# A planner's tables for a two-attention kernel: output products placed later, VectorE exps nearer to a phase's end, shared PSUM banks used sooner

## The chip, the cores and the metric

The kernel runs on one core of one Trainium2 chip. The metric is the device time of one execution in microseconds. Times are medians of several runs; a profile is of one execution, which has its own time.

## The reference

Two attention blocks read the same `x` (2048 rows, 512 columns) and are mixed by a gate that depends on the row. A has 32 query heads of width 16 on one shared key and value head; B has 32 full heads of width 16.

```python
g = sigmoid((x * gate_w).sum(-1, keepdims=True))
# A: q = x @ wq (32 heads of 16), k = x @ wk, v = x @ wv (one head of 16)
# B: q, k, v = split(x @ wqkv)     (32 heads of 16 each)
p = softmax(q @ k.T * 16 ** -0.5)  # for each head, 2048 x 2048
a, b = (p_A @ v_A) @ A_wo, (p_B @ v_B) @ B_wo
return g * a + (1 - g) * b
```

## The kernel before, in words

The exponentials of 2 x 32 x 2048 x 2048 scores are the bulk of the work. They are cut into **phases**: four groups of eight heads (`gi`), for each of them A and then B, two halves of the queries (`half`) and two pairs of head pairs (`q`): 32 phases, numbered from 0, of which 0 to 3 are A's, 4 to 7 B's, 8 to 11 A's, and so on. A phase has 32 **quads** of two **exps**, 64 exps in all, each of them 128 x 1024 elements.

One exp goes through these steps. TensorE makes its scores, 8 matmuls of 512 columns, into one of four PSUM tiles of two banks (`slots`). ScalarE reads it and writes exp into a tile in SBUF, `prob` or `vec` in the profile (L783, `exp`). When both exps of a quad are there, TensorE multiplies them with the values (L837, `values`) and adds up in the phase's own PSUM tile (`pair[0]`); a quad is multiplied whole (512 columns) or in two halves (256). The two tiles are then free again. When all 32 quads are in, VectorE copies the sum to SBUF (L905, in `emptied`), row sums go through DRAM to be inverted and spread (L648 to L673, `normalised`), and VectorE makes the normalised pair of 16-bit tiles `o16` (L681 to L687). `o16` has 8 buffers.

Part of the exps are made on VectorE instead (`vector_job`, `chain`): TensorE writes the scores into the shared PSUM tile (`pair[1]`), and VectorE works out a polynomial. For B that is a chain of three instructions (L1037, L1040, L1044) with two tiles, for A one of seven (L1004 to L1017) with three.

Other TensorE work shares `pair[1]`: projections of q, k and v for later phases (24 products each, with VectorE's evacuation at L487 and L490, and 16 DMAs on the SP and POOL queues at L422 that lay out q and k), and **output products** (`o_unit`): for each half and group, four units of 12 products of `o16` with the output weights, evacuated by VectorE (L599), and added to the output in DRAM by DMA. Those of the last group stay on the chip (L592).

The order of all this is fixed when the kernel is built. A planner inside the kernel (`_Plan`, `pe_step`) keeps a clock for each engine with costs from a table (`EXP`, `SCORES`, `HALF`, ...) and emits one instruction after another; on the chip each engine goes through its list in order and waits for semaphores. What the planner chooses hangs on these:

- `pick`: which exp VectorE gets next. While the exps left on ScalarE in this phase cost more than `CHAIN` and VectorE's own backlog, it is the last quad of this phase, otherwise the last one of the next phase.
- `vector_job`: the number of free tiles that it needs, `KEPT` of them a reserve; `spare_tiles` counts the free ones.
- `pe_step`: if more than `LEFT` tiles are free (`LEFT_END` near a phase's end), work in the shared tile goes first (`bursts`), otherwise products with the values.
- `due` times of projections and output products; a unit with the earliest goes first, and `hurry` holds back VectorE exps when `JOB` for each job leaves too little time.

After the last phase comes a **tail**: VectorE and ScalarE copy the last sum (L902, L903), ten DMAs move it about (L651), VectorE inverts and multiplies (L661, L679), and the last products and output DMAs follow.

Of the kernel before, what the change touches and what calls it, by code (L numbers as in the profile page):

```python
# [13 lines left out]
F16 = mybir.dt.float16  # L14
# [6 lines left out]
P = 128  # L21
# [26 lines left out]
SLACK, TIGHT, URGENT, SOON, AHEAD, LATER = 404, 404, 300, 500, 900, 3000  # L48
# [4 lines left out]
PROBS, VECS = 10, 6  # L53
LEFT, LEFT_END, KEPT, BEGIN = 3, 5, 3, 5
# [117 lines left out]
def _fast(ctx, tc, x, wq_a, wk_a, wv_a, wo_a, wqkv_b, wo_b, gate_w, out, flag):  # L172
# [397 lines left out]
    o16s = {}  # L570

    def o_unit(j, half, t, done, last):
# [16 lines left out]
        def finish(end):  # L589
            def take():  # L590
# [32 lines left out]
        due = 32 * (LASTS + half) if ends else 32 * (8 * j + 2 * half + 8)  # L623
        undone[j, half] = undone.get((j, half), 0) + 1
        return _Unit(jobs, finish, lambda now: all(made(("o16", n, half, q), math.inf) <= now and made(("wo", *groups[n]), math.inf) <= now for n, q in done)
# [4 lines left out]
    def normalised(n, half, q, raw, turned, now):  # L630
# [11 lines left out]
        if not ends:  # L642
# [4 lines left out]
            for which, count in heads:  # L647
                nc.sync.dma_start(held.rearrange("(e h) q -> h e q", e=2)[to : to + count], raw[which])  # L648
                to += count
        for m, (part, at, to, n_rows, e) in enumerate(moves):  # L650
            queues[m % len(queues)].dma_start(part[ROWS * e + to :][:n_rows], raw[at, e])  # L651
# [165 lines left out]
    def idle(now):  # L817
# [4 lines left out]
        return chained() > WORK + AHEAD + (EXTRA if half_vec else 0) or pick(now) is None or spare_tiles() < (0 if half_vec else KEPT) + 2  # L822
# [60 lines left out]
    def emptied(t):  # L883
# [16 lines left out]
        def take():  # L900
            if ph == LASTS:
                nc.vector.tensor_copy(state["raw"][:, 0], full[:, 0])  # L902
                nc.scalar.copy(state["raw"][:, 1], full[:, 1])  # L903
# [3 lines left out]
        def then(end):  # L907
# [4 lines left out]
            normalised(n, half, q, state["raw"], turned, end)  # L912
# [20 lines left out]
    def pick(now):  # L933
# [6 lines left out]
        need = CHAIN + plan.backlog(3)  # L940
# [11 lines left out]
    def pressing():  # L952
# [4 lines left out]
        return ph <= quads[min(at[0], len(quads) - 1)][0] and left_in(ph) * EXP < CHAIN  # L957
# [4 lines left out]
    def vector_job(now):  # L962
# [6 lines left out]
        if u is None or spare_tiles() < (3 if source(quads[u // 2][0]) == "a" else 2) + (0 if half_vec else 1 if source(quads[u // 2][0]) == "a" else KEPT):  # L969
            return None  # L970
# [735 lines left out]
```

## Time and profile before

| | |
|---|---|
| time, median of 3 runs (lowest, highest) | 1768.24 us (1766.13, 1768.64) |
| the profiled execution: its time, its span | 1765.05 us, 1763.3 us |
| TensorE matmul busy | 1712.2 us (97%) |
| ScalarE busy | 1703.4 us (97%); 1840 exps at L783 |
| VectorE busy | 1314.0 us (75%) |
| GpSimd busy | 190.8 us (11%) |
| mean granted TensorE clock | 0.995 |

The time stands 1.75 us above the span of the same execution, which is counted from the first to the last instruction. The profiled execution is 3.2 us faster than the median of the three runs. Busy time is a union: instructions of an engine that overlap are counted once. One L783 lasts 1117 ns in the mean, but the next begins before it ends. A row of the timeline gives the start, the duration to the end of the last of a group, the engine, the line, and in brackets how long the engine had been idle and what ended that.

### The profile page before, as it was taken

The page shows a single profiled execution, that of the slowest core. Times are in us where ns is not written, and L with a number is a line of the kernel's source. Part 1 is how long each engine was busy: PE and PEld are TensorE (multiplying, and loading weights), DVE is VectorE, ACT ScalarE, POOL GpSimd, SP SyncE. Part 2 cuts the span into 40 slices and gives each one's busy share as a digit, 9 for nine tenths or more (in the row PEclk, how much of TensorE's full clock was granted, in tenths as well). Part 3 has the DMA queues.
Part 4 walks back from the last instruction along what each step waited for, and adds up shares of the span by engine and source line. Part 5 has one row for each costly group of instructions (what it writes and reads, how often), then busy time and mean ns, then how long its engine had stood idle before and what let it go on. Part 6 is the DMA issues. An engine that isn't in the chain of part 4 may idle for free.

```text
span 1763.3 us, 108947 instructions
## 1 busy us (share of the span) xinstructions
PE 1712.2 (97%) x50939; PEld 983.3 (56%) x50939; DVE 1314.0 (75%) x1504; ACT 1703.4 (97%) x1855; POOL 190.8 (11%) x314
## 2 busy tenths in 40 slices
PE   8999999999999999999999999999999999999996
PEld 5556554565555565546565556555565555555553
DVE  5458699986748784997687785699587687498944
ACT  5999999999999999999999999999999999999994
POOL 1102000000000101001211211000211221100000
PEclk9999999999999999999999999999999999999998
DMA  5212110113111222112323222111322322111311
GB/s 151 62 41 65 52 38 19 41 35 76 45 50 48 54 67 62 28 31 53 52 53 65 52 60 58 47 28 41 71 35 52 59 59 71 39 35 28 109 62 64
DMA packets 71152, 95.10 MB, mean 54 GB/s; under 512 B 27581, under 2 KB 36061, under 8 KB 70693
## 3 DMA queue, kind: packets, MB, share of 16 engines
q1 hardware_dynamic: 53892, 58.61, 12.3%
q0 software_dynamic: 13568, 27.22, 7.6%
q8 instruction: 401, 6.57, 1.5%
q10 hardware_dynamic: 3232, 2.23, 0.4%
q14 instruction: 59, 0.48, 0.1%
HBM read 23.45 MB, written 17.81 MB: 23 GB/s over the span
## 4 chain that ended last, share of the span: by engine, by line
PE 67%; ACT 19%; DVE 7%; issue 3%; DMA 1%; SPq 1%; ACTq 0%; DVEq 0%
PE slot L837 34%; PE slot L752 20%; PE slot L215 12%; ACT prob L783 12%; ACT vec L783 7%; DVE prob L1037 1%; DVE prob L1040 1%; DVE prob L1017 1%; DVE prob L1044 1%; DVE vec L1044 0%; DVE vec L1037 0%; DVE prob L1004 0%; SPq L673 0%; PE slot L1395 0%; PE slot L309 0%
## 5 line engine op out<-in xcount | busy, mean ns | idle before, releaser
L783 ACT ACTIVATE prob<-slot 128x1024 f32<-128x1024 f32 x1118 | 1123.7, 1117 | 15.5 <-PE slot L752 14.4
L783 ACT ACTIVATE vec<-slot 128x1024 f32<-128x1024 f32 x712 | 749.9, 1119 | 5.3 <-PE slot L752 2.6
L837 PE MATMUL slot<-prob,vA 64*32 64x256 f32 (+1 forms) x7424 | 510.1, 451 | 0.1
L837 PE MATMUL slot<-prob,vB 64*32 64x256 f32 (+1 forms) x7480 | 499.8, 448 | 0.1
L752 PE MATMUL slot<-Qa,kA 64*32 64x512 f16 x8192 | 434.9, 379 | 6.6 <-DMA Qa<-loqa 2.2
L752 PE MATMUL slot<-Qb,K 64*32 64x512 f16 x8192 | 405.4, 379 | 25.0 <-ACT vec L783 9.7
L837 PE MATMUL slot<-vec,vB 64*32 64x256 f32 (+1 forms) x4840 | 373.9, 445 | 0.1
L837 PE MATMUL slot<-vec,vA 64*32 64x256 f32 (+1 forms) x4672 | 373.2, 445 | 0.2
L752 PEld LDWEIGHTS <-K 64*32 64x32 f16 x8192 | 187.2, 90 | 275.0 <-issue 212.4
L752 PEld LDWEIGHTS <-kA 64*32 64x32 f16 x8192 | 195.6, 90 | 247.7 <-issue 180.6
L837 PEld LDWEIGHTS slot<-prob,vA 64*32 64x32 f32 x7424 | 200.9, 106 | 42.3 <-issue 9.0
L837 PEld LDWEIGHTS slot<-prob,vB 64*32 64x32 f32 x7480 | 196.6, 106 | 48.4 <-issue 12.4
L837 PEld LDWEIGHTS slot<-vec,vB 64*32 64x32 f32 x4840 | 141.9, 106 | 27.5 <-issue 6.6
L837 PEld LDWEIGHTS slot<-vec,vA 64*32 64x32 f32 x4672 | 141.1, 106 | 26.6 <-issue 5.0
L1037 DVE TENSOR_SCALAR prob<-slot 128x1024 f32<-128x1024 f32 x92 | 112.7, 1225 | 19.8 <-PE slot L752 10.7
L1017 DVE SCALAR_TENSOR_TENSOR prob<-prob,prob 128x1024 f32<-128x1024 f32 x76 | 92.6, 1221 | 0.7
L1017 DVE SCALAR_TENSOR_TENSOR vec<-vec,prob 128x1024 f32<-128x1024 f32 x62 | 75.5, 1221 | 0.6
L215 PEld LDWEIGHTS <-o 64*32 64x32 f16 x3072 | 51.4, 93 | 36.2 <-ACT o L684 7.4
L1004 DVE TENSOR_SCALAR prob<-slot 128x1024 int32<-128x1024 f32 x42 | 51.3, 1222 | 26.7 <-PE slot L752 21.9
L215 PE MATMUL slot<-w16ob,o 64*32 64x512 f16 x1536 | 62.6, 387 | 7.9 <-ACT o L684 5.7
L905 DVE COPY prob<-slot 128x1024 f32<-128x1024 f32 x20 | 24.5, 1223 | 56.3 <-PE slot L215 35.4
L1044 DVE SCALAR_TENSOR_TENSOR prob<-prob,prob 128x1024 f32<-128x1024 f32 x54 | 66.1, 1226 | 0.3
(187 smaller groups left out, 1670.9 us busy)
## 6 DMA issues: line engine op xcount, KB each, us to landing
vB<-vB SPq DMA_DIRECT2D x32, 192.0 KB
prob<-back SPq DMA_DIRECT2D x160, 32.0 KB
out_dram<-prob POOLq DMA_DIRECT2D x40, 128.0 KB, 4.3
xT<-out_dram SPq DMA_DIRECT2D x16, 256.0 KB
out_dram<-vec POOLq DMA_DIRECT2D x24, 128.0 KB, 4.5
out_dram<-xT SPq DMA_DIRECT2D x12, 256.0 KB
vec<-back SPq DMA_DIRECT2D x88, 32.0 KB
vec<-in_A_x_dram SPq DMA_DIRECT2D x10, 256.0 KB
```

Of the source, the lines that this page charges most:

```text
L215: nc.tensor.matmul(outs[n : n + COLS, i], lhs[i][rows(i), n : n + COLS], rhs[i][rows(i)], start=start, stop=stop)
L752: nc.tensor.matmul(bank[a : a + COLS, hh], k[rows(hh), key : key + COLS], Q[src, gi, half, p][rows(hh), j * BLK : (j + 1) * BLK], start=Tr ...
L783: nc.scalar.activation(probs[u], sc, AF.Exp, scale=SCALE / (UP * UP))
L837: nc.tensor.matmul(pair[0][32 * k : 32 * k + 32, i, cols], v[rows(i)], probs[2 * m + k // 2][rows(i), hh, cols], start=first, stop=last)
L905: nc.vector.tensor_copy(state["raw"], full)
L1004: nc.vector.tensor_scalar(tile("p").bitcast(I32), pair[1], SCALE / (UP * UP) / math.log(2) * 2.0 ** 23, None, op0=ALU.mult)
L1017: nc.vector.scalar_tensor_tensor(p, m if i == 3 else p, VEC[i], m if i else w, op0=ALU.add, op1=ALU.mult)
L1037: nc.vector.tensor_scalar(tile("p"), pair[1], CUBE[0] * SCALE / (UP * UP), CUBE[1], op0=ALU.mult, op1=ALU.add)
L1040: nc.vector.scalar_tensor_tensor(tile("w"), tiles["p"], CUBE[2], tiles["p"], op0=ALU.add, op1=ALU.mult)
L1044: nc.vector.scalar_tensor_tensor(p, w, CUBE[3], p, op0=ALU.add, op1=ALU.mult)
```

## The change

It changes the planner's numbers and three of its rules:

- **Output products.** Their due time (all but the last group's) moves by three phases, from `8 * j + 2 * half + 8` to `+ 11`. Since `o16` tiles are then read later, `readers` counts the units that still have to read each, and VectorE's copy into a new `o16` (`high`) is not emitted before the tile's earlier content has been read.
- **VectorE exps.** `CHAIN` becomes 20000 for A and 7000 for B, from 24000 for both; `KEPT` becomes 1, from 3; for A the reserve of one tile is kept. `JOB` goes from 900 to 500.
- **Shared banks.** `LEFT` becomes 1, from 3: work in the shared tile goes first while two tiles or more are free. In the last phase it was 1 already.
- **Due times of projections**: q 8000 ahead of its phase instead of 14000, v 24000 instead of 18000; k and v may begin 12 quads later. `idle` loses `AHEAD`.
- **Tail.** The last sum is copied into two tiles, one for VectorE's half and one for ScalarE's.

```diff
-SLACK, TIGHT, URGENT, SOON, AHEAD, LATER = 404, 404, 300, 500, 900, 3000
+SLACK, TIGHT, URGENT, SOON, LATER = 404, 404, 300, 500, 3000
-PROBS, VECS = 10, 6
-LEFT, LEFT_END, KEPT, BEGIN = 3, 5, 3, 5
+PROBS, VECS, O16 = 10, 6, 8
+LEFT, LEFT_END, KEPT, BEGIN = 1, 5, 1, 5
...
+    def read16(k):
+        return k < 0 or readers.get(made16[k], 1) == 0
...
-        due = 32 * (LASTS + half) if ends else 32 * (8 * j + 2 * half + 8)
+        due = 32 * (LASTS + half) if ends else 32 * (8 * j + 2 * half + 11)
...
-                e = plan.vec(lambda c=c: high(c), 200, 3.3, 0.0, (b,), None, due)
+                e = plan.vec(lambda c=c: high(c), 200, 3.3, 0.0, (b,), None, due, room=lambda: read16(before))
...
-        return chained() > WORK + AHEAD + (EXTRA if half_vec else 0) or pick(now) is None or spare_tiles() < (0 if half_vec else KEPT) + 2
+        return chained() > WORK + (EXTRA if half_vec else 0) or pick(now) is None or spare_tiles() < (0 if half_vec else KEPT) + 2
...
             if ph == LASTS:
+                state["other"] = free_tiles.pop()
                 nc.vector.tensor_copy(state["raw"][:, 0], full[:, 0])
-                nc.scalar.copy(state["raw"][:, 1], full[:, 1])
+                nc.scalar.copy(state["other"][:, 1], full[:, 1])
...
-        need = CHAIN + plan.backlog(3)
+        need = CHAIN["ab".index(source(ph))] + plan.backlog(3)
...
-        if u is None or spare_tiles() < (3 if source(quads[u // 2][0]) == "a" else 2) + (0 if half_vec else 1 if source(quads[u // 2][0]) == "a" else KEPT):
+        if u is None or spare_tiles() < (3 if source(quads[u // 2][0]) == "a" else 2) + (0 if half_vec else KEPT):
...
-    CHAIN, EARLY = 24000, 12
-    JOB, AFTER, TURN, SPARE, WORK, EXTRA = 900, 3000, 3000, 5000, 1500, 7000
+    CHAIN, EARLY = (20000, 7000), 12
+    JOB, AFTER, TURN, SPARE, WORK, EXTRA = 500, 3000, 3000, 5000, 1500, 7000
...
-        bursts = begins and spare_tiles() > 1 or at[0] < len(quads) and spare_tiles() > (1 if at[0] >= 32 * LASTS else LEFT_END if ending else LEFT)
+        bursts = begins and spare_tiles() > 1 or at[0] < len(quads) and spare_tiles() > (LEFT_END if ending and at[0] < 32 * LASTS else LEFT)
...
-                                     lambda s=s: starts_in(64 * s) - 14000))
+                                     lambda s=s: starts_in(64 * s) - 8000))
...
-                        units.append(project(part, "b", gi, half, part + "_b", past(m - 22 + 10 * half),
-                                             lambda m=m, half=half, ns=14000 if part == "k" else 18000: starts_in(m + 128 + 16 * half) - ns))
+                        units.append(project(part, "b", gi, half, part + "_b", past(m - 10 + 10 * half),
+                                             lambda m=m, half=half, ns=14000 if part == "k" else 24000: starts_in(m + 128 + 16 * half) - ns))
```

What it does to the programs, counted in their instructions: ScalarE has 1820 exps instead of 1840. VectorE has 162 of B's chains instead of 142, and 66 of A's as before. TensorE does the same scores, products and projections; 42 more quads are multiplied in two halves instead of whole (336 more matmuls). GpSimd and SP have as many instructions as before. B's chains were 4 to 14 in a phase and are now 6 to 14. The table below is counted from the built orders: exps on VectorE in each phase of the four B blocks, and the number of ScalarE exps of the same phase that are still to come in the order when the scores of the phase's last VectorE exp are made.

| phases | VectorE exps before | after | still to come before | after |
|---|---|---|---|---|
| 4 to 7 | 8, 12, 12, 6 | 12, 12, 10, 10 | 29, 32, 33, 32 | 9, 7, 21, 15 |
| 12 to 15 | 4, 12, 12, 6 | 14, 6, 10, 12 | 30, 34, 34, 32 | 12, 14, 25, 3 |
| 20 to 23 | 4, 14, 12, 4 | 12, 6, 10, 12 | 32, 25, 25, 34 | 13, 11, 25, 3 |
| 28 to 31 | 4, 14, 10, 8 | 12, 6, 12, 6 | 32, 19, 33, 24 | 13, 13, 15, 23 |

VectorE's order where phase 15 ends (the last of a B block; `L905 COPY`, in the new numbering `L916 COPY`, is the copy of the phase's sum). L1004 to L1017 and, in the new numbering, L1015 to L1028 are A's chain; L599 is the evacuation of an output product. Before:

```order
L1017 SCALAR_TENSOR_TENSOR prob_101<-prob_101,vec_106 128x1024
L599 TENSOR_SCALAR prob_105<-slot_79 128x1024
L1004 TENSOR_SCALAR vec_108<-slot_79 128x1024
L1008 TENSOR_SCALAR prob_100<-vec_108 128x1024
L1012 TENSOR_SCALAR vec_111<-vec_108 128x1024
L1017 SCALAR_TENSOR_TENSOR vec_108<-prob_100 128x1024
L1017 SCALAR_TENSOR_TENSOR vec_108<-vec_108,prob_100 128x1024
L905 COPY prob_103<-slot_81 128x1024
```

After; L1048, L1051 and L1055 are B's chain:

```order
L1051 SCALAR_TENSOR_TENSOR prob_104<-vec_108 128x1024
L1055 SCALAR_TENSOR_TENSOR vec_108<-prob_104,vec_108 128x1024
L1048 TENSOR_SCALAR vec_110<-slot_79 128x1024
L1051 SCALAR_TENSOR_TENSOR prob_104<-vec_110 128x1024
L1015 TENSOR_SCALAR prob_101<-slot_79 128x1024
L1055 SCALAR_TENSOR_TENSOR vec_110<-prob_104,vec_110 128x1024
L1015 TENSOR_SCALAR prob_99<-slot_79 128x1024
L1019 TENSOR_SCALAR prob_96<-prob_101 128x1024
L1019 TENSOR_SCALAR vec_106<-prob_99 128x1024
L1023 TENSOR_SCALAR prob_104<-prob_101 128x1024
L916 COPY prob_97<-slot_81 128x1024
```

Before, the chains ahead of the copy belong to the next phase, A's; now the phase's own last chain ends five instructions ahead of the copy of its sum.

VectorE's order where phase 20 ends (the first of a B block). Before:

```order
L1037 TENSOR_SCALAR prob_98<-slot_80 128x1024
L1040 SCALAR_TENSOR_TENSOR prob_96<-prob_103 128x1024
L1040 SCALAR_TENSOR_TENSOR vec_106<-prob_98 128x1024
L905 COPY prob_99<-slot_81 128x1024
L1044 SCALAR_TENSOR_TENSOR prob_103<-prob_96,prob_103 128x1024
```

After; L605 is the evacuation of an output product, L691 to L697 make an `o16`:

```order
L691 TENSOR_TENSOR vec_107<-vec_107 128x256
L1048 TENSOR_SCALAR vec_111<-slot_81 128x1024
L1055 SCALAR_TENSOR_TENSOR prob_100<-vec_110,prob_100 128x1024
L1051 SCALAR_TENSOR_TENSOR prob_102<-vec_111 128x1024
L1055 SCALAR_TENSOR_TENSOR vec_111<-prob_102,vec_111 128x1024
L605 TENSOR_SCALAR vec_110<-slot_82 128x1024
L916 COPY prob_99<-slot_79 128x1024
L694 CAST o_26384<-prob_101 128x256 x2
```

The output products of a second half, which stood in the A phases ahead, now stand from the end of phase 19 to phase 21, and the `o16` copy (L694) comes after the product.

ScalarE's order at the end of the last phase. Before:

```order
L783 ACTIVATE vec_111<-slot_81 128x1024
L783 ACTIVATE prob_97<-slot_82 128x1024
L903 COPY prob_103<-slot_80 128x512
L651 DMA prob_100<-prob_103 32x512
L651 DMA prob_100<-prob_103 16x512 x2
```

After:

```order
L793 ACTIVATE vec_111<-slot_79 128x1024
L793 ACTIVATE prob_99<-slot_80 128x1024
L914 COPY prob_96<-slot_81 128x512
L659 DMA prob_103<-prob_101 32x512
L659 DMA prob_103<-prob_101 16x512
L659 DMA prob_103<-prob_96 16x512
```

VectorE's copy goes to `prob_103` before, as ScalarE's does, and to `prob_101` after, another tile than ScalarE's `prob_96`.

More of the change, by code (lines that the diff above doesn't have):

```diff
@@ L589, in finish @@
         def finish(end):
+            for n, q in done:
+                readers[n, half, q] -= 1
             def take():
@@ L622, in o_unit @@
         jobs = [(lambda k=k: job(k), PRODUCT) for k in range(len(steps))]
-        due = 32 * (LASTS + half) if ends else 32 * (8 * j + 2 * half + 8)
+        due = 32 * (LASTS + half) if ends else 32 * (8 * j + 2 * half + 11)
         undone[j, half] = undone.get((j, half), 0) + 1
+        for n, q in done:
+            readers[n, half, q] = readers.get((n, half, q), 0) + 1
         return _Unit(jobs, finish, lambda now: all(made(("o16", n, half, q), math.inf) <= now and made(("wo", *groups[n]), math.inf) <= now for n, q in done)
@@ L647, in normalised @@
             for which, count in heads:
-                nc.sync.dma_start(held.rearrange("(e h) q -> h e q", e=2)[to : to + count], raw[which])
+                nc.sync.dma_start(held.rearrange("(e h) q -> h e q", e=2)[to : to + count], raw[0][which])
                 to += count
         for m, (part, at, to, n_rows, e) in enumerate(moves):
-            queues[m % len(queues)].dma_start(part[ROWS * e + to :][:n_rows], raw[at, e])
+            queues[m % len(queues)].dma_start(part[ROWS * e + to :][:n_rows], raw[e][at, e])
         if not ends:
@@ L654, in normalised @@
         plan.sp = max(plan.sp, now) + (len(moves) + 3) * ISSUE_SP
-        returns.append((plan.sp + LANDS, raw))
-        o16 = ops.tile([P, 2, BLK], F16, tag="o16", name=f"o16{n}{half}{q}", bufs=8)
+        returns.append((plan.sp + LANDS, raw[0]))
+        o16 = ops.tile([P, 2, BLK], F16, tag="o16", name=f"o16{n}{half}{q}", bufs=O16)
         o16s[n, half, q] = o16
+        made16.append((n, half, q))
+        before = len(made16) - 1 - O16
         cut = P if ends else BLK // 2
@@ L911, in then @@
                 free["pv"] = end + FROM_VEC
-            normalised(n, half, q, state["raw"], turned, end)
+            normalised(n, half, q, [state["raw"], state.get("other", state["raw"])], turned, end)
             parts = [(m, r) for m, r in ((n - 1, 0), (n - 1, 2), (n, 0), (n, 2))]
@@ L956, in pressing @@
         ph = quads[half_vec[0] // 2][0]
-        return ph <= quads[min(at[0], len(quads) - 1)][0] and left_in(ph) * EXP < CHAIN
+        return ph <= quads[min(at[0], len(quads) - 1)][0] and left_in(ph) * EXP < CHAIN["ab".index(source(ph))]
     def chained():
```

2 lines of the change are left out of this document (1 added, 1 removed).

## The prediction

> **What bounds the kernel now.** I read the page's busy times first, then the busy time in windows of 100 us, then the groups and single stretches of the timeline. The page:
>
> ```profile
> span 1763.3 us, 108947 instructions
> PE 1712.2 (97%) x50939; PEld 983.3 (56%) x50939; DVE 1314.0 (75%) x1504; ACT 1703.4 (97%) x1855; POOL 190.8 (11%) x314
> ```
>
> TensorE and ScalarE are both at 97%, so the page alone doesn't say which one sets the pace. The windows do (columns: PE, PEld, DVE, ACT, POOL busy, then clock and DMA):
>
> ```profile
> 100.00:200.00 100.00, 99.37 (x3132) 59.08 (x3131) 76.59 (x91) 99.29 (x109) 10.40 (x18) 1.00 0.20 52
> 200.00:300.00 100.00, 97.99 (x2848) 54.17 (x2840) 87.34 (x93) 99.82 (x110) 8.53 (x16) 1.00 0.15 39
> 300.00:400.00 100.00, 95.93 (x2848) 55.29 (x2833) 90.04 (x94) 99.87 (x110) 4.69 (x9) 1.00 0.13 34
> ...
> 600.00:700.00 100.00, 98.81 (x3080) 60.55 (x3072) 61.95 (x75) 98.11 (x108) 14.18 (x26) 1.00 0.21 57
> ...
> 900.00:1000.00 100.00, 99.88 (x3064) 58.90 (x3056) 71.86 (x83) 99.94 (x110) 18.73 (x24) 1.00 0.28 55
> ...
> 1100.00:1200.00 100.00, 96.09 (x2749) 51.81 (x2733) 84.13 (x86) 99.93 (x110) 6.34 (x12) 1.00 0.13 35
> ```
>
> ScalarE does 108 to 110 exps in each 100 us and is idle for at most 2 us, also at 300 and at 1100 us, where TensorE has 300 matmuls fewer to do than at 900. An exp does not get shorter where TensorE has less work, so ScalarE is the bound. The same asked for phases 4 to 28 as one window, ScalarE's exps alone, then all engines in the last 61 us before the last values end:
>
> ```profile
> 256.00:1584.00 1328.00, 1322.25 (x1438) 1.00 0.21 50
> ...
> 1681.00:1742.00 61.00, 59.10 (x1760) 33.19 (x1759) 24.75 (x27) 53.54 (x58) 0.00 (x0) 1.00 0.13 39
> ```
>
> In the long window an exp costs 1328 / 1438 = 0.9235 us, waits included. In the last 61 us ScalarE is busy for 53.5 and TensorE for 59.1: there the bound is TensorE. How full TensorE really is, its jobs tell. From the timeline near the end:
>
> ```profile
> 1733.53 0.42 PE L752 MATMUL slot<-Qb,K 64*32 64x512 f16 x8
> 1733.75 0.85 PE L215 MATMUL slot<-w16oa,o 64*32 64x512 f16 x24
> 1734.40 0.41 PE L752 MATMUL slot<-Qb,K 64*32 64x512 f16 x8
> 1734.62 1.05 PE L837 MATMUL slot<-prob,vB 64*32 64x512 f32 x16
> 1735.48 0.41 PE L752 MATMUL slot<-Qb,K 64*32 64x512 f16 x8
> ```
>
> From start to start, the scores of an exp take 0.22 us, three products 0.65, a quad with the values 0.86: one job of 8 matmuls is 0.215 us, a quad is four of them. The built program has 2048 + 4 x 1024 + 1152 (projections and output products) = 7296 jobs, 1569 us, 89% of the span.
>
> **The change part by part.** *Twenty exps leave ScalarE.* 20 x 0.9235 = 18.5 us off the path; by the window at 900 us, where ScalarE never pauses, 20 x 100 / 110 = 18.2. I take 18.5.
>
> *They come to VectorE*, as twenty more of B's chains of three:
>
> ```profile
> 1657.96 1.22 DVE L1037 TENSOR_SCALAR prob<-slot 128x1024 f32<-128x1024 f32 x1
> 1659.09 1.22 DVE L1044 SCALAR_TENSOR_TENSOR vec<-vec,vec 128x1024 f32<-128x1024 f32 x1
> 1660.22 1.22 DVE L1040 SCALAR_TENSOR_TENSOR prob<-prob 128x1024 f32<-128x1024 f32 x1
> ```
>
> From start to start 1.13 us, so 20 x 3 x 1.13 = 68 us; VectorE goes from 1314 to 1382 us of about 1747 (79%). The window at 300 us ran at 90% without a loss on ScalarE. Cost 0, as long as the idle 21% lies where it is needed; the other case is the first rival.
>
> *TensorE's jobs* are the same ones. Forty-two quads are cut in two, which costs nothing: halves are two jobs each, as long as the whole. 0 us.
>
> *Where its jobs stand* changes. The windows with few matmuls (300 and 1100 us) lie in the first two phases of a B block, which had few projections and output products or none. In the last three blocks they get some, so TensorE is filled evenly. ScalarE's idle time in such windows is 0.07 to 0.18 us; in fuller ones it is 0.06 (at 900) to 1.89 (at 600). Six phases, some 300 us, become full: at least 0, at most 3 x 1.8 = 5.4 us. I take 1.1, nearer to the window at 900, since the fullest of these phases has 237 jobs to 58 exps, as phase 16 (884 to 937 us) had before.
>
> *Tiles.* With less reserve, an exp may need a tile whose last reader, a quad with the values, stands behind its own scores in TensorE's order. Fifteen exps did, 23 do. ScalarE's waits of before:
>
> ```profile
> ACT prob L783 <- PE slot L752: 14.4, 18, 5.9
> ...
> ACT vec L783 <- PE slot L837: 0.6, 3, 0.2
> ```
>
> Waits for values were 0.6 us in all, 0.2 the longest. Eight more cost 0.3 to 1.6 us by that row; two of the 23, in the last phase, have 5 and 8 jobs behind them, 1.1 and 1.7 us. I take 0.8, between 0 and 3.2.
>
> *The last phase.* Behind the 58th-last exp TensorE had 267 jobs left, now it has 271: 4 x 0.215 = 0.9 us in a stretch where it is the bound. Behind the 120th-last there are 13 more: at most 2.8. I take 0.9. [...]
>
> *The tail.* Two copies of the last sum follow each other:
>
> ```profile
> 1742.02 0.69 DVE L902 COPY prob<-slot 128x512 f32<-128x512 f32 x1 [9.90 <-PE slot L837]
> 1742.74 2.42 SPq L651 DMA_DIRECT2D prob<-prob  x4
> 1742.75 0.59 ACT L903 COPY prob<-slot 128x512 f32<-128x512 f32 x1 [5.64 <-DVE prob L902]
> ```
>
> ScalarE waits for VectorE only because both write one tile. With two, its copy starts some 0.7 us earlier, and the last of the DMAs with it, unless the issue of four DMAs on SP (2.42 us) holds them. Between 0 and -0.7; I take -0.4. The Trainium skill (PSUM — Partial Sum Buffer, "Specifications (TRN2)") gives both engines full bandwidth on PSUM at once when the banks differ, as these two do; no run here shows it.
>
> *Due times.* Q comes later, and nothing is added for it: see the second rival. The wait that the check of `o16` adds is one of the planner: VectorE's list holds the copy further back, and what stands behind it is in another order, not stopped.
>
> Sum: -18.5 + 1.1 + 0.8 + 0.9 - 0.4 = -16.1. The profiled execution of 1765.05 would come to 1749; its span to 1747.2. The median stands 3.2 us higher than that execution, so I predict 1768.24 - 16.1 = 1752 us.
>
> **The rivals.** *A phase's end waits for VectorE (slower).* The last VectorE exp of a B phase was scored 19 to 34 ScalarE exps before the phase's end, now it is 3 to 25 (the table of the change). In the orders, ten more of the B phases end on a quad that VectorE made. If VectorE is late there, the sum is closed late, and ScalarE, which is 2 to 9 exps into the next phase by then (14 after phase 30), runs out of tiles. VectorE is stopped by DMAs:
>
> ```profile
> DVE each L664 <- DMA each<-held: 13.9, 7, 4.3
> ...
> 1597.00 0.35 DVE L664 RECIPROCAL each<-each 128x32 f32<-128x32 f32 x1 [2.02 <-DMA each<-held]
> ...
> 1599.90 0.41 PE L752 MATMUL slot<-Qb,K 64*32 64x512 f16 x8 [1.77 <-DVE prob L1037]
> ...
> 1601.02 2.10 ACT L783 ACTIVATE prob<-slot 128x1024 f32<-128x1024 f32 x2 [1.52 <-PE slot L752]
> ```
>
> Seven waits, 2.0 us in the mean, and the one that ended at 1597 us did reach ScalarE, by way of a late chain and TensorE: 1.5 us. At 2.0 us for each of the ten ends it would cost 20, and 1772 comes out. It decides from 1.6 us an end on. Against it: seven in 32 phases is not ten in ten, an A phase's end is mostly of that kind already, and the window at 900 us, in A, is ScalarE's best. Chance 0.10.
>
> *Q lands late.* In the order, the last product of the queries for a B block's second half stood 73 or more exps ahead of their first score; in the blocks at phases 12, 20 and 28 it is 13, 23 and 22 now. The time they need, in the trace:
>
> ```profile
> L487 DVE TENSOR_SCALAR hiqb<-slot 128x1024 f16<-128x1024 f32 x8 | 9.8, 1222 | 19.1 <-ACT prob L783 12.7 <-PE slot L215 6.4
> ...
> 691.56 0.54 POOL L422 DMA_DIRECT2D Qb<-hiqb  x1 [12.38 <-DVE hiqb L487]
> ...
> 694.86 0.59 SPq L422 DMA_DIRECT2D Qb<-loqb  x1
> ...
> DMA to landing us min/median/max: 2.0/2.8/4.1
> ```
>
> VectorE's evacuation of 1.2 us ends as the first issue starts at 691.56, so the queries were through TensorE near 690; to 694.86 + 4.1 = 699 it is 9 us for the first two tiles, and 13 exps are 12 us. With 3 us of waiting on SP and POOL the first is late; all three, by 3 us each, give 1752 + 9 = 1761. Most of it speaks against: 22 exps are 20 us. Chance 0.14 for a gain of 3.5 to 10 us, by this or by full windows, tiles and the last phase at their upper ends (5.4, 3.2 and 2.8: also 1761).
>
> *TensorE takes over.* If 97% busy meant full, nothing would be gained: 1768. Against it are the 89% in jobs and the windows with fewer matmuls. Chance 0.08, with all else that ends within 0.2%.
>
> That the change does not do what it says is excluded: the 20 exps are counted.
>
> **How the numbers follow.** The forecast, a gain of 10 to 25 us, gets 0.68. With the second rival's 0.14 that is 0.82 for faster by more than 0.2% (3.5 us, about what a measurement of this kernel can tell from none); 0.08 within; 0.10 slower. The low end of the range: all 18.5, 0.7 of the tail and a third of the 14.4 us that ScalarE waited for scores, -24, so 1744. The high end: full windows at 5.4, tiles at 3.2, the last phase at 2.8 and one late Q at 3 give -18.5 + 14.4 = -4.1, so 1764; no change and slower lie beyond.
>
> **What the profile after would show.** The exp line with 1820 instructions and ScalarE's busy time down by about 18 us; 256 to 1584 us still at 0.92 us an exp; B's chains at 162 each; the windows in second phases of B with as many matmuls as the others. ScalarE's copy of the last sum would start with VectorE's. I am wrong if ScalarE's idle time grows by 10 us or more: behind scores with Qb (late Q), behind values or by VectorE's chains at the ends of B's phases.

## The result and the profile after

The changed kernel takes 1752.73 us (median of 4 runs, 1751.99 to 1753.65), the kernel before 1767.77 us (4 runs): 15.0 us less, ratio 0.9916, 95% interval [0.9899, 0.9933]. The forecast was 1752 us. The profiled execution of after has a span of 1750.1 us, 13.2 us less than the one of before; the rest of the difference is the spread of single executions. One execution in the whole study, of `short_both`, took 2120 us at a granted clock of 0.751, and the times and ratios below leave it out.

The page of after, busy times and the two groups of ScalarE's exps (count, busy and mean duration, then idle time ahead of them and what ended it):

```profile
span 1750.1 us, 110408 instructions
PE 1711.5 (98%) x51611; PEld 1006.9 (58%) x51611; DVE 1382.3 (79%) x1564; ACT 1685.4 (96%) x1835; POOL 192.4 (11%) x314
...
L793 ACT ACTIVATE prob<-slot 128x1024 f32<-128x1024 f32 x1100 | 1095.7, 1105 | 18.6 <-PE slot L762 14.5 <-PE slot L847 2.3 <-DVE vec L1051 0.3
L793 ACT ACTIVATE vec<-slot 128x1024 f32<-128x1024 f32 x710 | 736.0, 1105 | 6.8 <-PE slot L762 4.7 <-DVE xT L598 1.3 <-issue 0.3
```

ScalarE's busy time went from 1703.4 to 1685.4 us and VectorE's from 1314.0 to 1382.3. The 1810 exps here and ten whose tiles bear other names are the 1820. TensorE's busy time is as before, in a shorter span.

The windows that were shown of before, as far as they tell something, with the long one and the last 64 us before the last values end (columns as before: PE, PEld, DVE, ACT, POOL, clock, DMA):

```profile
300.00:400.00 100.00, 95.86 (x2658) 50.63 (x2648) 89.15 (x94) 99.34 (x110) 4.13 (x8) 1.00 0.14 34
...
700.00:800.00 100.00, 98.70 (x3036) 59.79 (x3027) 82.89 (x94) 98.79 (x108) 9.69 (x18) 1.00 0.25 64
...
900.00:1000.00 100.00, 99.65 (x3117) 57.85 (x3104) 79.87 (x93) 99.90 (x110) 13.39 (x18) 1.00 0.23 48
...
1100.00:1200.00 100.00, 98.87 (x3053) 60.22 (x3045) 79.07 (x90) 97.69 (x107) 17.53 (x26) 1.00 0.28 57
1500.00:1600.00 100.00, 98.96 (x3084) 60.65 (x3084) 77.12 (x89) 98.86 (x108) 19.99 (x28) 1.00 0.31 60
...
1665.00:1729.00 64.00, 62.30 (x1812) 36.43 (x1796) 32.17 (x34) 54.95 (x60) 0.00 (x0) 1.00 0.12 37
256.00:1584.00 1328.00, 1315.31 (x40120) 771.53 (x40119) 1098.70 (x1202) 1317.39 (x1433) 150.14 (x235) 1.00 0.22 49
```

In the long window an exp now costs 1328 / 1433 = 0.9267 us; it was 0.9235. That is 0.0032 x 1433 = 4.6 us of new waiting. The window at 1100 us shows where: the first two phases of a B block, which had 2749 matmuls in 100 us and 110 exps on ScalarE, have 3053 matmuls and 107 exps. The windows at 700 and 1500 us, in the other two late B blocks, look alike: ScalarE is idle for 1.2 and 1.1 us, at 1100 for 2.3. In the first B block (300 us), which got no output products, little changed: 2658 matmuls instead of 2848, and 0.66 us of idle time instead of 0.13.

Worked out from the starts of ScalarE's exps, phase by phase, these rows hold nearly all of the difference. The other phases are between 2.2 us shorter (phase 11) and 0.8 us longer at that price, and come to -0.4:

| stretch | before | after | at 0.9235 us an exp, after is |
|---|---|---|---|
| phases 12, 13, 20, 21, 28, 29 | 307.5 us for 332 exps | 308.8 us for 328 | 5.1 us too long |
| phases 30 and 31 | 104.6 us for 110 | 105.5 us for 110 | 1.0 us too long |
| phases 0 to 3 | 228.9 us for 244 | 227.6 us for 244 | 1.3 us shorter |
| first exp to last exp | 1708.3 us for 1840 | 1694.3 us for 1820 | 4.4 us too long |

So 20 x 0.9235 = 18.47 us less and 4.43 more, -14.0 between the first and the last exp; the first exp starts 0.7 us later, and from the last exp on there is 0.1 us more: -13.2.

Of the six phases of the first row, 12, 20 and 28 lost nothing against before (-0.2, +0.1 and -0.3 us), and 13, 21 and 29 lost 1.3, 3.2 and 0.9. Yet TensorE had no less to do in the first three: its matmuls in the trace, at the prediction's 0.215 us a job, fill 94 to 95% of phases 12, 20 and 28 and 89 to 92% of 13, 21 and 29.

### The profile page after: what moved, and what is told of

Read it like the earlier page. It is cut to its first block, busy times and chain, and to the rows that moved or that the text cites. A ratio compares the mean times of both kernels' runs of the same rounds, so it can differ in the third digit from the quotient of the medians.

```text
span 1750.1 us, 110408 instructions
## 1 busy us (share of the span) xinstructions
PE 1711.5 (98%) x51611; PEld 1006.9 (58%) x51611; DVE 1382.3 (79%) x1564; ACT 1685.4 (96%) x1835; POOL 192.4 (11%) x314
## 4 chain that ended last, share of the span: by engine, by line
PE 70%; ACT 19%; DVE 4%; issue 4%; DMA 1%; SPq 1%; ACTq 0%; DVEq 0%; POOL 0%
PE slot L847 36%; PE slot L762 21%; PE slot L215 12%; ACT prob L793 11%; ACT vec L793 8%; DVE prob L1048 1%; DVE vec L1028 0%; DVE prob L1028 0%; ACT early L793 0%; DMA each<-held 0%; PE slot L1406 0%; PE slot L309 0%; DVE vec L1048 0%; DMA Qa<-loqa 0%; DVE xT L1544 0%
## 5 line engine op out<-in xcount | busy, mean ns | idle before, releaser
L793 ACT ACTIVATE prob<-slot 128x1024 f32<-128x1024 f32 x1100 | 1095.7, 1105 | 18.6 <-PE slot L762 14.5
L793 ACT ACTIVATE vec<-slot 128x1024 f32<-128x1024 f32 x710 | 736.0, 1105 | 6.8 <-PE slot L762 4.7
L847 PE MATMUL slot<-prob,vB 64*32 64x256 f32 (+1 forms) x7824 | 523.3, 441 | 0.8 <-issue 0.7
L847 PE MATMUL slot<-prob,vA 64*32 64x256 f32 (+1 forms) x7544 | 483.3, 439 | 0.4 <-issue 0.4
L762 PE MATMUL slot<-Qb,K 64*32 64x512 f16 x8192 | 422.3, 379 | 13.1 <-ACT vec L793 3.1
L847 PEld LDWEIGHTS slot<-prob,vB 64*32 64x32 f32 x7824 | 210.7, 106 | 44.0 <-issue 8.3
L1048 DVE TENSOR_SCALAR prob<-slot 128x1024 f32<-128x1024 f32 x100 | 121.9, 1219 | 12.6 <-PE slot L762 9.9
L1028 DVE SCALAR_TENSOR_TENSOR prob<-prob,vec 128x1024 f32<-128x1024 f32 x73 | 88.6, 1219 | 0.5
L1028 DVE SCALAR_TENSOR_TENSOR prob<-prob,prob 128x1024 f32<-128x1024 f32 x71 | 86.6, 1221 | 0.8
L1048 DVE TENSOR_SCALAR vec<-slot 128x1024 f32<-128x1024 f32 x62 | 75.6, 1219 | 9.3 <-PE slot L762 6.6
L1015 DVE TENSOR_SCALAR prob<-slot 128x1024 int32<-128x1024 f32 x48 | 58.7, 1222 | 28.8 <-PE slot L762 25.6
L1051 DVE SCALAR_TENSOR_TENSOR prob<-prob 128x1024 f32<-128x1024 f32 x54 | 65.5, 1219 | 0.8
```

The source lines that it names most:

```text
L762: nc.tensor.matmul(bank[a : a + COLS, hh], k[rows(hh), key : key + COLS], Q[src, gi, half, p][rows(hh), j * BLK : (j + 1) * BLK], start=Tr ...
L793: nc.scalar.activation(probs[u], sc, AF.Exp, scale=SCALE / (UP * UP))
L847: nc.tensor.matmul(pair[0][32 * k : 32 * k + 32, i, cols], v[rows(i)], probs[2 * m + k // 2][rows(i), hh, cols], start=first, stop=last)
L1015: nc.vector.tensor_scalar(tile("p").bitcast(I32), pair[1], SCALE / (UP * UP) / math.log(2) * 2.0 ** 23, None, op0=ALU.mult)
L1028: nc.vector.scalar_tensor_tensor(p, m if i == 3 else p, VEC[i], m if i else w, op0=ALU.add, op1=ALU.mult)
L1048: nc.vector.tensor_scalar(tile("p"), pair[1], CUBE[0] * SCALE / (UP * UP), CUBE[1], op0=ALU.mult, op1=ALU.add)
```

## The experiments

Medians are compared by their ratio to the kernel before on the same chip. After has 0.9916.

### One engine's work cut at a time

My theory was the prediction's: ScalarE alone sets the pace. Four kernels each take work from one engine and leave the order as it is.

*Forty of ScalarE's exps, two in each of phases 8 to 27, over half the columns:*

```diff
...
-        nc.scalar.activation(probs[u], sc, AF.Exp, scale=SCALE / (UP * UP))
...
+        to, src = (probs[u][:, 0], sc[:, 0]) if 8 <= ph < 28 and exps_in[ph] in (16, 32) else (probs[u], sc)
+        nc.scalar.activation(to, src, AF.Exp, scale=SCALE / (UP * UP))
```

> The changed kernel with 40 of its ScalarE exps (two in each of phases 8 to 27) done on 512 of 1024 columns; the other half of those tiles keeps what it held. The order of everything is that of the changed kernel. By the times of 512 and 1024 columns in the trace (590 and 1105 ns) ScalarE has 40 x 0.5 = 20 us less to do. Theory 1, ScalarE sets the pace outside the last phase: 12 to 20 us shorter than the changed kernel, 1733 to 1741 (less than all 20 because TensorE fills up). Theory 2, TensorE at 98% busy sets the pace: 0 to 3 us shorter, about 1751. Theory 3, late VectorE chains at the ends of B's phases set it: under 6 us shorter.

Measured: 1755.58 us, 0.9928 [0.9909, 0.9948]: nothing gained. ScalarE did get less to do, and waited instead:

```profile
PE 1714.7 (98%) x51611; PEld 1008.3 (57%) x51611; DVE 1382.5 (79%) x1564; ACT 1676.1 (95%) x1835; POOL 191.6 (11%) x314
...
ACT prob L797 <- PE slot L763: 20.8, 34, 5.8
ACT vec L797 <- PE slot L763: 10.4, 25, 1.7
```

9.3 us less busy (I had expected twice that: a short exp costs more than half a long one), and 31.2 us of waiting for scores where after has 19.2: 12.0 us more. So a little less work on ScalarE alone, spread as single exps, is worth nothing in the changed kernel, and the theory fell here.

*Half the values of forty quads left out (17.2 us of TensorE):*

```diff
+            short = 8 <= quads[m][0] < 28 and put_in[0] in (8, 16)
-            values(m, slice(n, n + wide))
+            if n + wide == BLK // 2 or not short:
+                values(m, slice(n, n + wide))
+            elif n == 0:
+                values(m, slice(0, BLK // 2))
```

> The changed kernel with half of the columns left out of 40 quads' products with the values (two quads in each of phases 8 to 27), same order. TensorE has 40 x 0.43 = 17.2 us less to do. Theory 1 (ScalarE): 0 to 4 us shorter, 1749 to 1753. Theory 2 (TensorE): about 17 us shorter, 1736. Theory 3 (VectorE's chains): 0 to 2 us shorter.

Measured: 1750.47 us, 0.9914 [0.9899, 0.9929]: nothing either. TensorE alone isn't the bound.

*The third instruction of each of B's 162 chains over half the columns:*

```diff
-                nc.vector.scalar_tensor_tensor(p, w, CUBE[3], p, op0=ALU.add, op1=ALU.mult)
+                nc.vector.scalar_tensor_tensor(p[:, 0], w[:, 0], CUBE[3], p[:, 0], op0=ALU.add, op1=ALU.mult)
```

> The changed kernel with the third instruction of all 162 of B's chains on 512 of 1024 columns, same order. VectorE has 162 x 0.53 = 86 us less to do, and every chain of B is ready earlier. Theory 1 (ScalarE): 0 to 3 us shorter, 1750 to 1753. Theory 2 (TensorE): no change. Theory 3 (a B phase's end waits for VectorE; fourteen such ends): 6 to 20 us shorter, 1733 to 1747.

Measured: 1752.46 us, 0.9925 [0.9909, 0.9941]. VectorE was busy for 1304.0 us instead of 1382.3, less than before the change, and the time did not move. How long VectorE is busy holds up nothing that the time shows; its waits for DMAs stay in this run as they were.

*Sixty-eight of the 84 products of the last group's output units left out (14.6 us of TensorE):*

```diff
+            if ends and k not in (0, len(steps) - 1):
+                return
```

> The changed kernel with 68 of the 84 output products of the last group left out (the first and the last of each unit stay), same order; 68 x 0.215 = 14.6 us less for TensorE, nearly all of it in the last phase. Theory 1 with TensorE as the bound of the last phase: 3 to 6 us shorter, 1747 to 1750, since ScalarE's 58 exps, 53 us, and 6 us of values behind them are next. If ScalarE bounds the last phase too: 0 to 1 us shorter. Theory 2 (TensorE everywhere): about 14 us shorter, 1738.

Measured: 1755.08 us, 0.9931 [0.9914, 0.9948], no gain; the last phase became 0.2 us shorter, with ScalarE's longest wait in it, 2.1 us for a tile, as in after. The prediction's reading that TensorE bounds the last phase is not borne out.

### Which part of the change, and how far it goes

*After, with the output products due as before:*

```diff
-        due = 32 * (LASTS + half) if ends else 32 * (8 * j + 2 * half + 11)
+        due = 32 * (LASTS + half) if ends else 32 * (8 * j + 2 * half + 8)
```

> The changed kernel with the due time of the output products as before (+ 8 instead of + 11). The planner then keeps 1836 exps on ScalarE instead of 1820. Theory 1, what counts is the number of exps left on ScalarE at 0.92 us each, as long as TensorE's jobs are spread evenly: 15 us of the gain are lost, a ratio to the kernel before of 0.998 (between 0.996 and 1.001). Theory 2, the gain comes from VectorE exps near the phases' ends and from the shared banks, with the due time a side matter: a ratio near that of the changed kernel, 0.992.

Measured: 1762.74 us, 0.9981 [0.9972, 0.9991]. The planner then leaves 1836 exps on ScalarE: four fewer than before, at 0.9235 us 3.7 us, ratio 0.9979.

*Before, with the later output products and the check of `o16` alone:*

```diff
-        due = 32 * (LASTS + half) if ends else 32 * (8 * j + 2 * half + 8)
+        due = 32 * (LASTS + half) if ends else 32 * (8 * j + 2 * half + 11)
...
-                e = plan.vec(lambda c=c: high(c), 200, 3.3, 0.0, (b,), None, due)
+                e = plan.vec(lambda c=c: high(c), 200, 3.3, 0.0, (b,), None, due, room=lambda: read16(before))
```

> The kernel before with the later due time of the output products alone, and the check of their tiles. The planner has 1830 exps on ScalarE instead of 1840. Theory 1 (0.92 us for each exp): 9 us shorter, a ratio of 0.995 (0.993 to 0.997). Theory 2 (due time a side matter): no change, 1.000.

Measured: 1755.31 us, 0.9931 [0.9915, 0.9948], with 1830 exps. One part of the change brings some 0.69 of the 0.84%. With the due times of q alone, or of k and v alone, set back, the built order is the same as after's, instruction for instruction: in the changed kernel either of those parts does nothing by itself.

*After, with the planner driven further*, to 1810 exps:

```diff
-LEFT, LEFT_END, KEPT, BEGIN = 1, 5, 1, 5
+LEFT, LEFT_END, KEPT, BEGIN = 0, 4, 0, 4
```

> The changed kernel with other numbers: LEFT, LEFT_END, KEPT, BEGIN = 0, 4, 0, 4. The planner has 1810 exps on ScalarE, ten fewer, and 266 jobs of TensorE behind the 58th-last exp instead of 271. Theory 1: 9 to 10 us shorter than the changed kernel, a ratio to the kernel before of 0.986. Theory 3, ScalarE and TensorE are both full already after the change, so fewer exps only bring waits for scores: 0 to 3 us shorter, about 0.991.

Measured: 1755.23 us, 0.9939 [0.9923, 0.9956]. *To 1798 exps:*

```diff
-LEFT, LEFT_END, KEPT, BEGIN = 1, 5, 1, 5
+LEFT, LEFT_END, KEPT, BEGIN = 0, 4, 1, 6
...
-        due = 32 * (LASTS + half) if ends else 32 * (8 * j + 2 * half + 11)
+        due = 32 * (LASTS + half) if ends else 32 * (8 * j + 2 * half + 13)
...
-    CHAIN, EARLY = (20000, 7000), 12
-    JOB, AFTER, TURN, SPARE, WORK, EXTRA = 500, 3000, 3000, 5000, 1500, 7000
+    CHAIN, EARLY = (24000, 7000), 12
+    JOB, AFTER, TURN, SPARE, WORK, EXTRA = 300, 3000, 3000, 5000, 1500, 9000
```

> The changed kernel with other numbers that push output products into the last phase: due + 13, CHAIN for A 24000, LEFT, LEFT_END, KEPT, BEGIN = 0, 4, 1, 6, JOB 300, EXTRA 9000. ScalarE has 1798 exps, 22 fewer; behind the 58th-last exp TensorE has 321 jobs instead of 271. Theory 1 by the count alone: 20 us shorter than the changed kernel, 0.980 of the kernel before. Theory 1 with TensorE as the bound of the last phase: 22 x 0.92 = 20 less 50 x 0.215 = 11, so 9 us shorter, 0.9865. Theory 3 (both full): no shorter than the changed kernel, 0.992 or above.

Measured: 1787.39 us, 1.0120 [1.0100, 1.0139], slower than before. ScalarE's timeline where phase 15 ends, and its largest waits:

```profile
873.70 1.02 ACT L793 ACTIVATE vec<-slot 128x1024 f32<-128x1024 f32 x1
907.31 1.02 ACT L793 ACTIVATE prob<-slot 128x1024 f32<-128x1024 f32 x1 [32.59 <-PE slot L762]
909.44 1.94 ACT L793 ACTIVATE vec<-slot 128x1024 f32<-128x1024 f32 x2 [1.11 <-DMA Qa<-loqa]
...
ACT prob L793 <- PE slot L762: 52.2, 19, 32.6
ACT o L694 <- DVE prob L689: 28.9, 4, 25.5
```

ScalarE stands for 32.6 us because projections and output products were put off until the next phase's Q wasn't there. TensorE worked some of them off meanwhile and then stood too, for 8.4 us that the profile puts down to a DMA. And a last `o` is 25.5 us in coming where it was 4.5; the products put off until then are the likely reason. The long wait is of the kind of the prediction's second rival, though before an A block and not inside a B block.

*To 1814 exps* (the first number is what the planner counts for an exp):

```diff
-EXP, EXP_ENDS, EXP_AFTER = 916, 1148, 456
+EXP, EXP_ENDS, EXP_AFTER = 925, 1148, 456
```

> The kernel after with one number of the planner changed, the time it gives to an exp (925 in place of 916): 1814 exps on ScalarE in place of 1820, with as many jobs of TensorE behind the 58th-last exp as in the kernel after or fewer. If ScalarE set the pace, six exps less would give 6 x 0.925 = 5.5 us: ratio to the kernel before 0.9885. If both engines are full together, as with 1810 exps, nothing is gained: 0.990 to 0.993.

Measured: 1748.27 us, 0.9897 [0.9878, 0.9917]. It is the fastest whole kernel of the study, but its interval overlaps after's, so that it beats after is not shown. The expectation had 0.9885 for ScalarE alone as the bound and 0.990 to 0.993 for both engines; the interval holds both, so this run doesn't decide.

Exps on ScalarE against the ratio, with what 0.9235 us an exp would give:

| exps | ratio | at 0.9235 us an exp |
|---|---|---|
| 1836 | 0.9981 [0.9972, 0.9991] | 0.9979 |
| 1830 | 0.9931 [0.9915, 0.9948] | 0.9948 |
| 1820 (after) | 0.9916 [0.9899, 0.9933] | 0.9895 |
| 1814 | 0.9897 [0.9878, 0.9917] | 0.9864 |
| 1810 | 0.9939 [0.9923, 0.9956] | 0.9843 |

Down to 1830 the gain keeps up with the rule (at 1830 it is larger, with the rule at the end of the interval). From 1820 on the rule lies outside the intervals, and the gain falls behind. These kernels differ in more than the count, since the planner makes another order each time.

### Both engines, or the ring of score slots?

Two readings were left: ScalarE and TensorE are both full, so that what one is spared it spends waiting for the other; or only the ring of score slots (two of the four PSUM tiles, since the pair takes two) swallows a short exp, because the next scores wait for the slot of the exp before it. Or a third limit holds both.

*Both exps of forty quads in phases 8 to 27 short*, 80 in all (`halved` names two quads of each phase):

```diff
...
-        nc.scalar.activation(probs[u], sc, AF.Exp, scale=SCALE / (UP * UP))
+        to, src = (probs[u][:, 0], sc[:, 0]) if halved(u // 2) else (probs[u], sc)
+        nc.scalar.activation(to, src, AF.Exp, scale=SCALE / (UP * UP))
```

> The kernel after, but both exps of 40 quads (two quads in each of phases 8 to 27) are taken on ScalarE over 512 columns in place of 1024: 80 shorter exps, some 0.43 us each, 34 us of ScalarE's busy time; the scores, the values and VectorE's work stay. The other half of those probabilities is left as it was in the tile. Theory 1 (ScalarE and TensorE are full together, so that less work on one alone only makes it wait for the other): at most 4 us gained against the kernel after, ratio to the kernel before 0.989 to 0.992, and ScalarE's idle time before exps grows from 25 us to 55 or more. Theory 2 (only the ring of two score slots swallows a single short exp, because the next scores were released by the exp before it; a second short exp in a row shows): about half, 40 x 0.43 = 17 us gained, ratio 0.982. Theory 3 (ScalarE alone sets the pace, as the prediction had it): 34 us, ratio 0.972.

Measured: 1748.67 us, 0.9902 [0.9886, 0.9917]: some 2.5 us of the 23.5 that left ScalarE.

*The same with half the scores and half the values of those quads left out too:*

```diff
...
-        products(u, sc)
+        products(u, sc, 1 if halved(u // 2) else 2)
...
```

> As the kernel with pairs of short exps, and in the same 40 quads half of the scores (512 of 1024 columns of both exps) and half of the values are left out too: 120 jobs, 120 x 0.215 = 26 us of TensorE at the same places where 34 us leave ScalarE. Theory 1 (both full together): now 18 to 26 us are gained against the kernel after, ratio to the kernel before 0.977 to 0.981. Theory 2 (the ring of slots): the same 17 us as with the pairs of short exps alone, or some 5 more, ratio 0.979 to 0.982, and no difference of more than 6 us between the two kernels. Theory 4 (a third limit, such as VectorE or the DMAs, holds both engines): neither kernel gains, 0.991 twice.

Measured: 1746.99 us, 0.9891 [0.9873, 0.9909], no difference from `short_pairs` that the intervals show. It looked like a third limit. ScalarE at one of those quads:

```profile
994.24 0.71 ACT L804 ACTIVATE vec<-slot 128x512 f32<-128x512 f32 x1
995.01 0.60 ACT L804 ACTIVATE prob<-slot 128x512 f32<-128x512 f32 x1
995.97 1.02 ACT L804 ACTIVATE vec<-slot 128x1024 f32<-128x1024 f32 x1 [0.36 <-PE slot L772]
```

After the second short exp, ScalarE waits for scores. A quad's values stand in TensorE's order only when its exps are done, so TensorE was relieved some exps after the place where ScalarE was. With so few slots ahead, a relief at another place may not count. That was an argument, and it stays one: the last run relieves TensorE everywhere in a phase, but also of far more, some 206 us in sixteen phases against 26 in twenty, so it doesn't tell place from amount.

*TensorE relieved over whole phases (8 to 23), with and without short exps* (as in `short_pairs`, but four quads in each of phases 8 to 15 and 24 to 27):

```diff
...
-            values(m, slice(n, n + wide))
+            if not (8 <= quads[m][0] < 24 and 0 < put_in[0] < QUADS - 1):
+                values(m, slice(n, n + wide))
+            elif n == 0:
+                values(m, slice(0, BLK // 2))
```

> The kernel after with two things left out in different stretches, so that one run has all four cases. In phases 8 to 23 half of the values of every quad but the first and the last of a phase is left out (2 of 4 jobs; 16 x 30 x 0.43 = 206 us of TensorE). In phases 8 to 15 and 24 to 27 both exps of four quads a phase are taken over 512 columns (8 a phase; the kernel with pairs measured 23.5 / 80 = 0.29 us of ScalarE each). So: 0 to 7 as in the kernel after, 8 to 15 both (64 short exps, 19 us), 16 to 23 TensorE relieved alone, 24 to 27 short exps alone (32, 9 us). Theory 1 (ScalarE and TensorE are both full, and what is taken from one is waited for the other): phases 16 to 23 lose only what ScalarE waited there, 3 to 8 us; phases 24 to 27 lose 1 to 3 of their 9; phases 8 to 15 lose 19 us and the waits too, 20 to 27. Ratio to the kernel before 0.970 to 0.978. Theory 2 (the ring of two score slots swallows short exps, however free TensorE is): 8 to 15 lose no more than 16 to 23, 3 to 8 us each; ratio 0.981 to 0.987. Theory 4 (a third limit such as VectorE): no stretch of B's phases (12 to 15, 20 to 23) loses anything, ratio 0.985 to 0.992.

Measured: 1730.99 us, 0.9804 [0.9788, 0.9821]. That lies between what the expectation gave for the two full engines and for the ring, and its interval reaches the ring's, so the whole time doesn't decide; the stretches have to. The three stretches in after (phases 8 to 15, 16 to 23, 24 to 27):

```profile
452.00:872.00 420.00, 417.51 (x13060) 254.35 (x13048) 350.52 (x385) 416.36 (x452) 39.76 (x68) 1.00 0.22 53
872.00:1294.00 422.00, 419.15 (x12807) 246.16 (x12792) 344.13 (x380) 418.06 (x455) 61.27 (x92) 1.00 0.24 51
1294.00:1513.50 219.50, 218.78 (x6716) 125.46 (x6700) 175.53 (x197) 218.79 (x239) 30.43 (x46) 1.00 0.22 50
```

And in this kernel, the same work on ScalarE and VectorE by its counts:

```profile
450.00:855.20 405.20, 353.19 (x10741) 185.36 (x10727) 349.34 (x384) 394.68 (x452) 39.50 (x68) 1.00 0.23 54
855.20:1273.50 418.30, 359.10 (x10776) 184.84 (x10776) 343.46 (x379) 416.72 (x455) 60.07 (x92) 1.00 0.24 51
1273.50:1491.00 217.50, 216.28 (x6684) 128.90 (x6684) 175.66 (x197) 209.38 (x239) 30.11 (x46) 1.00 0.22 51
```

| phases | left out | length against after |
|---|---|---|
| 16 to 23 | TensorE's values alone, some 103 us of jobs | -3.7 us |
| 24 to 27 | ScalarE alone, 32 short exps, 9.4 us busy | -2.0 us |
| 8 to 15 | both, with 64 short exps, 21.7 us busy | -14.8 us |

In the second row of after ScalarE had 422.0 - 418.06 = 3.9 us of idle time to lose; with TensorE relieved 418.3 - 416.72 = 1.6 are left. Short exps alone gave 2.0 of 9.4 us. Together they gave 14.8, where twice the second case and the first make 7.7. That is the mark of two engines that are both full, and it excludes a third limit of both in phases 8 to 15, VectorE above all: it was busy there for 350.5 us in after and for 349.3 here, and the stretch became shorter all the same.

These stretches are of one execution of each kernel, and where nothing differs they spread too. Phases 28 to 31 are the same in both kernels and took 2.2 us longer here; phases 0 to 7 took 423.4 to 426.7 us in seven of the profiled kernels (after, `short_exp`, `short_values`, `short_last`, `short_pairs`, `short_both`, `relief`), whose order and work are the same there. So -2.0 and -3.7 are hardly more than the spread. The 14.8 is well clear of it, and its distance from 7.7 is twice as large as it; 32 short exps alone in the same phases 8 to 15 (`short_pairs`) gave nothing, 419.9 us as in after.

The ring may have a part in it: after a short exp the next one started 0.72 us later in phases 8 to 15 (mean, 0.94 at the same places in after) and 0.84 in phases 24 to 27, so even beside a free TensorE not all of the 0.29 us came through, and 14.8 is below the 20 to 27 expected.

## Why the prediction was right, step by step

*Twenty exps off ScalarE, -18.5.* ScalarE's busy time fell by 18.0 us and the exps were paid as said. But the reason given, that ScalarE is the bound because an exp doesn't get shorter where TensorE has less to do, was half of it. It fits before, whose second-phase windows left TensorE free (216 and 315 matmuls fewer at 300 and 1100 us than at 900, not 300 in both), though no run cut an engine's work in before. It is the later output products that used this room: with them alone 1830 exps and 0.9931, without them 0.9981. In phases 8 to 15 of after, where both were tried, ScalarE and TensorE hold each other; in the whole kernel ten exps fewer brought nothing, and six fewer no gain that is clear of the spread.

*VectorE, 68 us, cost 0.* The busy time came out as worked, 1382, and the run with 78 us less on VectorE shows that the busy time costs nothing that can be measured.

*Filled phases, +1.1 between 0 and 5.4.* This term was mis-sized: 5.1 us, near the upper end, and 6.6 in `short_last`, which has the same order there. In both, all of it is in phases 13, 21 and 29 and none in 12, 20 and 28, which are no less full. So the number of TensorE's jobs doesn't give the price; single waits of ScalarE have to be looked at. Here is what the profile shows around two of the largest in phase 29 (us in all, times, longest), first at 1576 to 1580 us and then at 1598 to 1603:

```profile
DVE each L674 <- DMA each<-held: 3.6, 1, 3.6
...
PE slot L762 <- DVE vec L1048: 1.0, 1, 1.0
ACT prob L793 <- PE slot L762: 1.0, 1, 1.0
...
ACT prob L793 <- PE slot L762: 1.1, 1, 1.1
...
PE slot L847 <- issue: 0.7, 1, 0.7
```

The first is a late VectorE chain, as in the prediction's first rival; two such waits, 0.57 and 0.98 us, lie in these phases, but before had one of 1.52 there, so they make up next to nothing of the 5.1. The second follows a pause in which TensorE waited for nothing that the profile shows ("issue"). There are four waits of that kind in these phases, 3.0 us together, and none in the same phases of before; the three largest, 0.70, 0.85 and 1.13 us, follow pauses of 0.57, 0.56 and 0.73 us. The prediction's upper end has in the main the same origin: 1.15 of the 1.89 us in the window at 600 us of before follow such a pause.

```profile
652.12 0.40 PE L752 MATMUL slot<-Qa,kA 64*32 64x512 f16 x4 [0.96 <-issue]
...
652.62 1.03 ACT L783 ACTIVATE prob<-slot 128x1024 f32<-128x1024 f32 x1 [1.15 <-PE slot L752]
```

From phase 4 to the last exp the trace of after has six such pauses of TensorE, and that of before this one. What they are, and why there are more of them, no run shows; that the filled phases leave no room to absorb them is likely, but not shown either.

*Tiles, +0.8 between 0 and 3.2.* ScalarE's waits for values were 0.6 us before. Now:

```profile
ACT prob L793 <- PE slot L847: 2.3, 2, 2.1
ACT vec L793 <- PE slot L847: 0.2, 1, 0.2
...
1682.96 1.03 ACT L793 ACTIVATE prob<-slot 128x1024 f32<-128x1024 f32 x1 [2.11 <-PE slot L847]
```

1.9 us more, and nearly all of it one wait in the last phase, one of the two places that the prediction named (with 1.1 and 1.7).

*Last phase, +0.9.* Phases 30 and 31 are 1.0 us longer, but that is 1.5 less in phase 30 and 2.4 more in phase 31. That the size fits is luck, and the reason doesn't fit: 14.6 us less of TensorE's output products shortened the last phase by 0.2, and the wait of 2.1 us for a tile, already counted under the tiles, is most of the 2.4. The Trainium skill (Perfetto Trace Analysis, "Identifying the Most-Contended Engine") judges TensorE's headroom by the share of peak FLOPs and by the busy share of weight loads. By the second, after has 58%, and yet TensorE holds ScalarE back in phases 8 to 15; the first was not worked out.

*Tail, -0.4 between 0 and -0.7.* It came to nothing:

```profile
1728.65 0.69 DVE L913 COPY prob<-slot 128x512 f32<-128x512 f32 x1 [9.74 <-PE slot L847]
1729.37 2.42 SPq L659 DMA_DIRECT2D prob<-prob  x4
1729.38 0.59 ACT L914 COPY prob<-slot 128x512 f32<-128x512 f32 x1 [5.70 <-DVE prob L913]
```

ScalarE's copy still begins when VectorE's has ended, with two tiles to write to as with one. By the profile it still waits for it; what the two copies share now is the PSUM tile that they read. So the wait "only because both write one tile" was wrong. Whether the two could run side by side, no run shows.

*Not foreseen:* phases 0 to 3 are 1.3 us shorter, and the first exp is 0.7 us later.

The terms came to -16.1 in the prediction; the difference is -13.2 between the profiled executions and -15.0 between the medians. The sum was right because its one large term was; that 1752 is within 1 us of the median is luck, since the profiled executions miss the sum by 2.9 us. ScalarE's idle time, span less busy time, grew by 4.8 us, from 59.9 to 64.7, short of the 10 us at which the prediction called itself wrong.

*The rivals.* A phase's end waited for VectorE, but for little: ScalarE stood for 0.33 us behind VectorE's chains where phase 15 ends and where phase 23 ends, the two phases with 3 exps still to come, and not for 2.0 us at ten ends. VectorE's waits for the DMA fell from seven to three. Two of them reached ScalarE inside a phase, the one in phase 29 shown above, and one in phase 21, by way of a VectorE chain that started late (L1048 after the inversion at L674). Its 0.57 us are the first of the two waits below; ahead of the second, TensorE paused:

```profile
868.39 4.69 ACT L793 ACTIVATE prob<-slot 128x1024 f32<-128x1024 f32 x5 [0.33 <-DVE prob L1051]
...
1290.41 1.02 ACT L793 ACTIVATE prob<-slot 128x1024 f32<-128x1024 f32 x1 [0.33 <-DVE vec L1051]
...
DVE each L674 <- DMA each<-held: 9.3, 3, 3.6
...
1153.64 0.35 DVE L674 RECIPROCAL each<-each 128x32 f32<-128x32 f32 x1 [3.15 <-DMA each<-held]
...
1155.88 2.08 ACT L793 ACTIVATE vec<-slot 128x1024 f32<-128x1024 f32 x2 [0.57 <-PE slot L762]
...
1159.87 1.03 ACT L793 ACTIVATE vec<-slot 128x1024 f32<-128x1024 f32 x1 [0.85 <-PE slot L762]
```

Q did not land late in after: TensorE waits for no DMA of Qb. Where the planner is pushed to 1798 exps it does, for 2.8 us. And "TensorE takes over", the rival with the smallest chance, has some truth: not for these twenty exps, but for what comes after them, and then together with ScalarE.

## What to carry to other kernels

Two engines that are both busy for 96% and more can hold each other: before costing a further gain by one of them alone, cut the work of each by itself, and then of both over a whole stretch; only the third tells whether the other is in the way. A cut of both at forty single quads showed nothing here. Work that is moved from the bound engine pays as long as the other engine has room in the same stretch, so look for windows with fewer instructions of that engine, and for work that can be moved into them. Before the idle time of a window becomes the price of filling another one, look at what ended each wait in it. Here waits behind pauses of TensorE made up more than half of it, and phases that were no less full cost nothing.

## What the hardware showed

- In `short_pairs` an exp over 512 columns took 645 ns in the mean (641 where it wrote a `prob`) and freed 23.5 / 80 = 0.29 us of ScalarE, not half of the 0.92 us that an exp over 1024 columns takes. In `short_exp` it was 9.3 / 40 = 0.23, and beside the relieved TensorE 21.7 / 64 = 0.34:

```profile
L804 ACT ACTIVATE vec<-slot 128x1024 f32<-128x1024 f32 x673 | 690.9, 1086 | 13.2 <-PE slot L772 11.3 <-issue 0.2 <-PE slot L858 0.2
...
L804 ACT ACTIVATE vec<-slot 128x512 f32<-128x512 f32 x37 | 23.8, 645 | 2.8 <-PE slot L772 1.8 <-ACT prob L804 0.2
```

- TensorE's busy time follows its load only in part: where some 103 us of values were left out of phases 16 to 23, it fell from 419.15 to 359.10 us, by 60.
- TensorE paused now and then, for 0.22 to 0.73 us in after and once for 0.96 us in before, with nothing in the profile that it waited for. Behind all of these but one of 0.22 us, ScalarE stood for somewhat longer than the pause, 0.28 to 1.15 us. Ahead of scores and values, after had five of them (us in all, times, longest):

```profile
PE slot L762 <- issue: 1.4, 3, 0.6
PE slot L847 <- issue: 1.2, 2, 0.7
```
